# A new written-out order for the end of a one-core attention and maxout kernel, and five smaller final stores in place of four

## The chip, the core and the metric

The kernel runs on one core of a Trainium2 chip. The metric is the device time of one execution in microseconds (us), as the median of several runs. Engines are named as in the profile: PE (TensorE), DVE (VectorE), ACT (ScalarE), POOL (GpSimd) and SP (SyncE, which here only issues transfers). Each engine works through its own list of instructions in order.

## The reference

Attention with positive features for 8 batches of 8 heads, 576 tokens and head size 64, and after it a maxout layer on all 4608 tokens. Cut to what matters:

```
proj = einsum('bhsd,df->bhsf', x, w_phi); proj -= max(abs(proj), -1)
phi  = concat(exp(proj), exp(-proj))                 # for q and for k
attn = (q_p @ (k_p^T @ v)) / (q_p . sum(k_p) + 1e-6)
x    = attn as 4608 x 512
h    = maximum(maximum(x @ w1, x @ w2), x @ w3)      # 512 -> 768
out  = h @ w_out                                     # 768 -> 512, float32
```

## The kernel before

**The work.** The attention is made in 16 units (a batch and four of its heads each). Their results `xT` lie with the 512 channels on partitions, brought there by a transposing DMA (line 703). The maxout layer is done in nine blocks of 512 tokens (`chunk`, line 832): blocks 0 to 7 are the first 512 tokens of the batches, and block 8 is made of the last 64 tokens of all eight batches, which POOL copies together into `x_last` (line 965). The layer is rewritten: with the differences w2 - w1 and w3 - w1, h is x @ w1 + max(0, x @ (w2 - w1), x @ (w3 - w1)), so that the output is x @ (w1 @ w_out) + hT @ w_out.

**One block.** Six `up` and six `up2` products (line 848; 128 x 512 each, four matmuls) give the two differences for six slices of 128 hidden channels. An `up` result is clipped at zero out of PSUM into `hT` by ACT (line 857) or by DVE (line 859); an `up2` result is combined with it by a maximum on DVE (line 855). Then comes the output product, with an inner size of 512 + 768 = ten slices of 128.

**Blocks 5 to 8** make the output product with seven products of half size in place of eight (`fast`, line 742). POOL forms four sums or differences of quarters of x (128 x 512) and four of `hT` (128 x 768), all at line 760. PE then makes seven products p1 to p7 of ten matmuls each (line 795, 128 x 256), and the output block of 512 x 512 is put together out of PSUM: ACT or DVE copies p1 (line 808), and DVE makes seven additions (line 802) in the tiles `low` (tokens 0 to 255 of the block) and `high` (tokens 256 to 511), both of the pool `raw`, and in a temporary tile `osb`. A quarter is called c11 (low, columns 0 to 255), c12 (low, 256 to 511), c21 and c22 (high). The steps are: osb = p6 + p1; c21 = p7 + osb; c12 = p5 + osb, then + p3; c22 = p5 + c21; c21 = c21 + p4; c11 = p1 + p2. c22 must be made before p4 is added into c21.

**The stores.** The rows of blocks 0 to 7 leave as two DMAs of 64 x 512 float32 (128 KB) for each 128 tokens, all issued by SP; that is eight DMAs for a block. Block 8 leaves as four DMAs of 128 x 512 (256 KB), two issued by SP and two by ACT (line 827). A store waits for both column halves of its rows.

**The order.** Nothing is left to a scheduler when the program is built: every step (a node) has a number, and the string `PLAN` lists for each node its engine, a planned start and the buffer slots it takes (`154T5@38.05` is node 154 on PE in PSUM bank 5). `plan` (line 259) reads it, and each engine issues its nodes in that order. T is PE, D is DVE, A is ACT, G is POOL and S is SP. The planned starts only sort the steps; the engines wait for each other by semaphores. `fill` (line 277) puts idle matmuls into planned gaps of PE.

Of the kernel before, what the change touches and what calls it, by code (L numbers as in the profile page):

```python
# [233 lines left out]
1004T21@224.97 1050A@225.22 1058T4@225.29 1008T5@225.51 1005D0@225.54 1393G3@225.55 1051A@225.73 1064T160@225.93 1009D1@226.16
1060A@226.21 1059A@226.72 1061T7@227.06 1006T2@227.18 1056A@227.20 1066D@227.22 1391G5@227.28 1052T3@227.50 1065D@227.60
1002T4@227.72 1053A@227.97 1007D0@227.98 1353T5@228.04 1054A@228.47 1003D1@228.60 1062A@228.96 1392G@229.03 1399T0@229.13
1063A@229.32 1010S@229.37 1057A@229.66 1069T60@230.22 1073T2@230.54 1470G@230.76 1070D0@230.79 1071T3@230.86 1362S@230.87
1394G@231.16 1406T4@231.18 1072D1@231.43 1074D0@232.05 1067T7@232.27 1397T6@232.59 1068D1@232.84 1075S@233.61 1408T1@233.68
1395T3@234.77 1401T2@235.86 1396D0@236.11 1398D2@236.74 1404T7@236.95 1440G4@237.04 1409D@237.38 1400D7@238.00 1420T3@238.04
1472G@238.24 1403D@238.64 1497G5@238.66 1418T6@238.91 1407D@239.28 1477T1@239.78 1438G@239.86 1402D@239.90 1413S@240.05  # L240
1421D0@240.52 1422T0@240.65 1499G@241.06 1419D@241.13 1416T4@241.52 1423D@241.77 1439G@242.26 1405D@242.38 1424T2@242.39
1417A@242.64 1411S@243.15 1475T3@243.26 1498G@243.46 1425A@243.51 1436T6@244.13 1410S@244.35 1441G@244.66 1432T0@245.00
1412S@245.55 1500G@245.86 1489T7@245.87 1433D@246.12 1414T4@246.74 1437D@246.74 1434T0@247.61 1415A@247.86 1476A1@248.36
1426T2@248.48 1430T4@249.35 1427D@249.60 1491T6@250.22 1431D@250.47 1354D@251.09 1481T3@251.09 1435D@251.71 1359S@251.86
1428T2@251.96 1482A@252.21 1478D@252.33 1483T4@252.83 1360S@253.06 1429D@253.08 1487T5@253.70 1444G1@253.85 1484A@253.95
1361S@254.26 1493T0@254.57 1488D@254.82 1490D@255.44 1473T1@255.44 1442G3@255.58 1494D@256.06 1479T2@256.31 1474D@256.68
1495T3@257.18 1443G@257.33 1480A@257.43 1485T4@258.05 1492D@258.08 1450T5@258.92 1445G@259.08 1486D@259.17 1496D@259.79
1452T7@260.01 1501G0@260.81 1455T0@261.10 1459T1@262.19 1502G@262.56 1446T2@263.28 1503G1@264.29 1448T6@264.37 1447A7@264.62
1505T4@265.46 1449D0@265.71 1504G@266.02 1451D6@266.35 1457T3@266.55 1506A2@266.80 1460D@266.97 1454D@267.59 1511T2@267.64
1458D@268.23 1507T6@268.73 1453D@268.85 1464S@269.00 1456D@269.49 1509T5@269.82 1508D3@270.11 1463S@270.20 1512D@270.75  # L250
1516T1@270.91 1510D3@271.37 1462S@271.40 1518T4@272.00 1513D@272.01 1461S@272.60 1517D@272.65 1514T3@273.09 1519D@273.34
# [50 lines left out]
def kernel(  # L302
# [439 lines left out]
    def fast(b, ready, hT, evac, out_rows, ff, n_out):  # L742
# [46 lines left out]
        def product(a, w, s):
            ps = bank("fps", [P, 2, HF])  # L790

            def mm(ps=ps, a=a, w=w):
                for p in range(2):
                    for c in range(5):
                        nc.tensor.matmul(ps()[:, p, :], lhsT=a(c, p), rhs=w(c), start=(p + c == 0), stop=(p + c == 5))  # L795
# [4 lines left out]

        def add(ps, need, out, other, bufs):
            return ff("fa", {"DVE": 0.62}, lambda: nc.vector.tensor_tensor(out(), ps()[0](), other(), ALU.add),  # L802
                      need + [ps()[1]], [ps()[0]] + bufs, locks=[ps()[0]])
# [17 lines left out]
        n_11 = add(lambda: p2, [n_u], c11, c11, [low])
        for tt in range(SM // P):
            o2, need = (low, [n_11, n_12]) if tt < 2 else (high, [n_21, n_22])

            def store(n_, pieces, tt=tt, o2=o2):
                for dram_ap, rows in pieces:
                    queue_of[n_.eng].dma_start(dram_ap, o2()[rows, tt % 2, :])
# [183 lines left out]
```

## Time and profile before

| what | value |
|---|---|
| median of 3 runs | 282.27 us (281.68 to 282.67) |
| the profiled execution | 282.29 us, of which its span is 280.5 us |
| busy in the span: PE, DVE, ACT, POOL | 97%, 80%, 68%, 60% |
| granted PE clock | 0.996 of full speed |
| matmul instructions | 3663 |

The span runs from the first to the last instruction of the profiled execution, and 1.79 us of that execution's own time lie outside it. Times in the profile count from the start of the span. An instruction row gives start, duration, engine, line, and output<-input; a q behind an engine's name is its sequencer, which is busy while it issues a DMA. In rows of stretches, the columns are the busy time of each engine with the number of instructions begun there, then the granted clock of PE, the mean busy share of the 16 DMA engines, and GB/s.

### The profile page before, as it was taken

How to read it: one execution, taken by the hardware profiler on the slowest of the kernel's cores; microseconds unless marked ns; L12 is line 12 of the kernel's file. 1: busy time of each engine (PE TensorE's matmuls, PEld its weight loads, DVE VectorE, ACT ScalarE, POOL GpSimd, SP SyncE). 2: the span in 40 equal slices, each digit the busy share in tenths (PEclk: the TensorE clock that was granted, in tenths of full speed). 3: DMA queues.
4: the chain of work that ended last, by engine and by line, in shares of the span. 5: the costliest groups of instructions: out<-in, count | busy, mean ns of one | idle time of the engine just before them, and what ended most of it. 6: DMA issues, size and time to landing. Idle time of an engine off the chain costs nothing.

```text
span 280.5 us, 8829 instructions
## 1 busy us (share of the span) xinstructions
PE 270.9 (97%) x3663; PEld 164.1 (58%) x3663; DVE 224.0 (80%) x466; ACT 191.3 (68%) x439; POOL 168.5 (60%) x147
## 2 busy tenths in 40 slices
PE   8899999999999999999999999999999999999991
PEld 3566774465546555564556456565485589444881
DVE  4899899988869997889898878897589565756292
ACT  3799997798879988898684699887654860112000
POOL 8075787839444764570768079267875892927910
PEclk9999999999999999999999999999999999999998
DMA  7999999997999997799899729984232108245037
GB/s 212 234 211 320 266 224 197 384 277 139 287 382 245 197 313 251 193 204 227 240 263 156 194 49 261 202 201 89 51 78 49 40 18 118 55 95 116 0 89 212
DMA packets 68050, 51.46 MB, mean 183 GB/s; under 512 B 48746, under 2 KB 52650, under 8 KB 68010
## 3 DMA queue, kind: packets, MB, share of 16 engines
q1 hardware_dynamic: 63561, 45.41, 66.2%
q0 software_dynamic: 4000, 4.92, 10.3%
q8 instruction: 28, 0.46, 0.6%
q10 hardware_dynamic: 449, 0.57, 0.6%
q14 instruction: 12, 0.10, 0.1%
HBM read 34.64 MB, written 9.44 MB: 157 GB/s over the span
## 4 chain that ended last, share of the span: by engine, by line
PE 78%; DMA 9%; DVE 6%; ACT 3%; issue 1%; POOL 1%; DVEq 0%; POOLq 0%; ACTq 0%
PE ups L848 33%; PE fps L795 8%; PE ops L884 7%; PE psn L673 5%; PE kvps L655 5%; PE ops L879 5%; PE psq L547 5%; PE psm L626 5%; DMA qk_bf<-in_k_dram 3%; DMA qkT<-qk_bf 3%; DMA qkT<-mT 3%; ACT Eq L639 2%; DVE raw L802 2%; PE pm L950 2%; PE tps L509 1%; DVE mqp L566 1%
## 5 line engine op out<-in xcount | busy, mean ns | idle before, releaser
L601 POOL TENSOR_TENSOR vab<-raw,em 128x1152 bf16<-128x1152 f32 (+1 forms) x36 | 68.1, 1906 | 69.4 <-ACT em L597 55.1
L560 ACT ACTIVATE Ek<-psk 128x512 bf16<-128x512 f32 (+1 forms) x160 | 82.2, 568 | 13.8 <-PE psk L547 10.0
L848 PE MATMUL ups<-xT,w_bf 128*128 128x512 bf16 x384 | 90.8, 379 | 0.0
L639 ACT ACTIVATE Eq<-psm 128x512 bf16<-128x512 f32 (+1 forms) x160 | 79.4, 571 | 10.4 <-PE psm L626 9.6
L848 PEld LDWEIGHTS <-w_bf 128*128 128x128 bf16 x432 | 41.0, 98 | 46.4
L566 DVE TENSOR_REDUCE mqp<-psq 128x4 bf16<-128x512 f32 (+1 forms) x80 | 49.2, 634 | 8.4 <-PE psk L547 5.7
L566 DVE TENSOR_REDUCE mk<-psk 128x4 f32<-128x512 f32 (+1 forms) x80 | 48.9, 630 | 1.1 <-ACT Ek L560 0.5
L855 DVE TENSOR_TENSOR hT<-hT,ups 128x512 bf16<-128x512 bf16 x54 | 36.2, 684 | 16.8 <-PE ups L848 13.9
L857 ACT ACTIVATE hT<-ups 128x512 bf16<-128x512 f32 x28 | 16.6, 606 | 30.1 <-PE ups L848 30.0
L680 DVE TENSOR_TENSOR x_sb<-psn,rden 128x320 bf16<-128x320 f32 x64 | 31.5, 492 | 2.2
L492 POOL CAST qk_bf<-raw 128x1152 bf16<-128x1152 f32 x24 | 27.2, 1148 | 5.8 <-DMA qkT<-qk_bf 3.5
L673 PEld LDWEIGHTS <-Eq 128*128 128x128 bf16 x640 | 24.7, 97 | 7.5 <-ACT Eq L639 0.7
L884 PE MATMUL ops<-wout_bf,hT 128*128 128x512 bf16 x120 | 29.1, 379 | 0.0
L673 PE MATMUL psn<-kv_sb,Eq 128*128 128x65 bf16 x640 | 26.8, 194 | 0.5 <-ACT Eq L639 0.5
L547 PE MATMUL psq<-w,qkT 64*128 64x128 bf16 x288 | 24.5, 217 | 1.0 <-DMA qkT<-qk_bf 0.6
L547 PE MATMUL psk<-w,qkT 64*128 64x128 bf16 x288 | 24.1, 217 | 0.2
L547 PEld LDWEIGHTS <-qkT 64*128 64x128 bf16 x576 | 16.6, 94 | 12.7 <-issue 8.9
L626 PE MATMUL psm<-qkT,wphi_m 128*128 128x512 bf16 (+1 forms) x70 | 22.3, 359 | 0.5 <-DMA qkT<-mT 0.3
L879 PE MATMUL ops<-xT 128*128 128x512 bf16 x80 | 20.6, 380 | 0.0
L859 DVE TENSOR_SCALAR hT<-ups 128x512 bf16<-128x512 f32 x26 | 17.5, 684 | 3.8 <-PE ups L848 3.6
L655 PE MATMUL kvps<-vab,Ek 64*128 64x65 bf16 x1152 | 20.2, 190 | 0.0
L655 PEld LDWEIGHTS <-Ek 64*128 64x128 bf16 x1152 | 18.8, 94 | 2.3 <-DVE mk L566 0.4
(97 smaller groups left out, 333.8 us busy)
## 6 DMA issues: line engine op xcount, KB each, us to landing
raw<-in_v_dram SPq DMA_DIRECT2D x16, 576.0 KB
raw<-in_q_dram SPq DMA_DIRECT2D x12, 576.0 KB
raw<-in_k_dram SPq DMA_DIRECT2D x12, 576.0 KB
out_dram<-osb SPq DMA_DIRECT2D x40, 128.0 KB
out_dram<-raw SPq DMA_DIRECT2D x24, 128.0 KB
w_bf<-in_moe_w_dram POOLq DMA_DIRECT2D x3, 768.0 KB, 9.4
qk_bf<-in_q_dram POOLq DMA_DIRECT2D x3, 288.0 KB, 8.2
qk_bf<-in_k_dram POOLq DMA_DIRECT2D x3, 288.0 KB, 9.3
```

Of the source, the lines that this page charges most:

```text
L547: nc.tensor.matmul(ps()[:, i, :], lhsT=cols[r, :], rhs=w2[r, c, :], start=True, stop=True)
L560: nc.scalar.activation(Ek[s]()[:, tiles_of(t0, n), :], of(1), EXP, scale=1.0 - 2.0 * s)
L566: nc.vector.tensor_reduce((mq, mk)[c]()[:, tiles_of(t0, n)], of(c), AXX, ALU.max, apply_absolute_value=True)
L601: (nc.vector if n_.eng == "DVE" else nc.gpsimd).tensor_tensor(vab()[:, g, t0:t1, 0:D], vb()[:, t0:t1, :], em()[:, g, t0:t1].unsqueeze(2).t ...
L626: nc.tensor.matmul(psm()[:, 0:w], lhsT=wphi_m, rhs=rhs, start=True, stop=True)
L639: nc.scalar.activation(Eqb()[s][:, cols], psm()[:, 0:w], EXP, scale=1.0 - 2.0 * s)
L655: nc.tensor.matmul(kvps[ab]()[:, t // NT, g, :], lhsT=Ek[g]()[r, t, :], rhs=vab()[r, g, t, :], start=(t + g == 0), stop=(t == UT - 1 and g ...
L673: nc.tensor.matmul(psn()[:, c, :], lhsT=Eqb()[g][:, t0:t0 + P], rhs=kv()[:, pr, ab, g, :], start=(g == 0), stop=(g == 1))
L848: nc.tensor.matmul(ups(), lhsT=w_bf[i + 1][:, ct, j * P:(j + 1) * P], rhs=tokens_of(ct), start=(ct == 0), stop=(ct == CT - 1))
L855: nc.vector.tensor_tensor(hT()[:, j, :], hT()[:, j, :], ups(), ALU.max)
L879: nc.tensor.matmul(ops_()[:, 0:width], lhsT=tile_of(ct, tt), rhs=line_w[:, ct, cols], start=(ct == 0), stop=False)
L884: nc.tensor.matmul(ops_()[:, 0:width], lhsT=hT()[:, j, tt * P:(tt + 1) * P], rhs=wout_bf[:, j, cols], start=False, stop=(j == JT - 1))
```

## The change

The change writes the plan anew from 225 us on (orders and buffer slots), and divides the end of block 8. In earlier parts of the string only three pairs of nodes with equal or nearly equal starts on different engines change places. There are three kinds of edits:

- The order of blocks 7 and 8. Before, their `up` and `up2` products were mixed; now block 7 is finished first, `up` and `up2` alternate, and all twelve clips out of PSUM are on ACT (before, ACT had seven of them and DVE five). Block 7's seven products come as p1 (ahead of the last `up2` of block 8), p6, p5, p3, p2, p7, p4, and block 8's as p1, p2, p6, p7, p5, p3, p4 (before p1, p5, p6, p7, p4, p2, p3).
- In block 8, p4 is made as two products of five matmuls, one for each 128 tokens, in two PSUM banks, and is added to c21 in two additions of 128 x 256.
- Block 8 leaves in five DMAs by column halves: c11, c12 and c22 as 128 x 2 x 256 (256 KB in rows of 1 KB), and c21 as two of 128 x 256 (128 KB). Each waits for its own additions alone.

```diff
-1522A@273.42 1523S@273.80 1515D@274.43 1520S@275.20 1521A@275.20
+1518T1@273.82 1515D@273.84 1524A@273.99 1517D@274.53 1523S@274.68 1519D@274.95 1525A@275.10 1526S@275.52
...
-        def product(a, w, s):
-            ps = bank("fps", [P, 2, HF])
+        def product(a, w, s, halves=(0, 1)):
+            ps = bank("fps", [P, len(halves), HF])
...
-                for p in range(2):
+                for k, p in enumerate(halves):
                     for c in range(5):
-                        nc.tensor.matmul(ps()[:, p, :], lhsT=a(c, p), rhs=w(c), start=(p + c == 0), stop=(p + c == 5))
+                        nc.tensor.matmul(ps()[:, k, :], lhsT=a(c, p), rhs=w(c), start=(k + c == 0),
+                                         stop=(k == len(halves) - 1 and c == 4))
...
-        p4 = product(a_of(1, 1), t_of(3), None)
-        n_21 = add(lambda: p4, [n_7, n_22], c21, c21, [high])
+        n_21 = []
+        for halves in ((0,), (1,)) if b == B else ((0, 1),):
+            p4 = product(a_of(1, 1), t_of(3), None, halves)
+
+            def c21_of(halves=halves):
+                return high()[:, halves[0]:halves[-1] + 1, 0:HF]
+            n_21.append(add(lambda p4=p4: p4, [n_7, n_22], c21_of, c21_of, [high], 0.07 + 0.28 * len(halves)))
...
-        for tt in range(SM // P):
-            o2, need = (low, [n_11, n_12]) if tt < 2 else (high, [n_21, n_22])
+        parts = [(low, 0, 2, 0, HF, n_11), (low, 0, 2, HF, DM, n_12), (high, 0, 2, HF, DM, n_22),
+                 (high, 0, 1, 0, HF, n_21[0]), (high, 1, 2, 0, HF, n_21[-1])]
+        for o2, p0, p1_, c0, c1, need in parts if b == B else []:
+            def last(n_, o2=o2, p0=p0, p1_=p1_, c0=c0, c1=c1):
+                whole = out.rearrange("(r c) n -> c r n", c=NT)[NT - 1]
+                t0 = HT * (o2 is high)
+                queue_of[n_.eng].dma_start(whole[t0 + p0 * P:t0 + p1_ * P, c0:c1].rearrange("(t p) n -> p t n", p=P),
+                                           o2()[:, p0:p1_, c0:c1])
+            n_ = ff("store", {"SP": 0.6, "ACT": 0.6}, None, [need], [o2], pipe=0.5 * (p1_ - p0), lat=1.5, packet=100.0)
+            n_.fn = lambda n_=n_, f=last: f(n_)
+        for tt in range(0 if b == B else SM // P):
+            o2, need = (low, [n_11, n_12]) if tt < 2 else (high, n_21 + [n_22])
```

DVE's last seven additions before, all of block 8. Here raw_5731 is `low`, raw_5789 is `high` and osb_5773 the temporary; the fps tiles are the products in PSUM:

```order
L802 TENSOR_TENSOR osb_5773<-fps_5747,raw_5731 128x512
L802 TENSOR_TENSOR raw_5731<-fps_5735,osb_5773 128x2x256
L802 TENSOR_TENSOR raw_5789<-fps_5762,osb_5773 128x2x256
L802 TENSOR_TENSOR raw_5789<-fps_5735,raw_5789 128x2x256
L802 TENSOR_TENSOR raw_5789<-fps_5778,raw_5789 128x2x256
L802 TENSOR_TENSOR raw_5731<-fps_5793,raw_5731 128x2x256
L802 TENSOR_TENSOR raw_5731<-fps_5808,raw_5731 128x2x256
```

DVE's last eight now, with raw_5751 as `low`, raw_5793 as `high` and osb_5779 as the temporary:

```order
L803 TENSOR_TENSOR osb_5779<-fps_5755,raw_5751 128x512
L803 TENSOR_TENSOR raw_5751<-fps_5740,raw_5751 128x2x256
L803 TENSOR_TENSOR raw_5793<-fps_5768,osb_5779 128x2x256
L803 TENSOR_TENSOR raw_5751<-fps_5782,osb_5779 128x2x256
L803 TENSOR_TENSOR raw_5793<-fps_5782,raw_5793 128x2x256
L803 TENSOR_TENSOR raw_5751<-fps_5796,raw_5751 128x2x256
L803 TENSOR_TENSOR raw_5793<-fps_5809,raw_5793 128x256
L803 TENSOR_TENSOR raw_5793<-fps_5815,raw_5793 128x256
```

c11 (the addition of p2) has moved from the sixth place to the second, and the last two rows are the two halves of c21 in place of c11 and c12.

SP's last stores before; raw_5718 and raw_5702 are `high` and `low` of block 7, raw_5789 and raw_5731 those of block 8, and the first two rows belong to blocks 5 and 6:

```order
L827 DMA out_0_dram<-raw_4799 64x512 x4
L827 DMA out_0_dram<-raw_4903 64x512 x2
L827 DMA out_0_dram<-raw_5718 64x512 x4
L827 DMA out_0_dram<-raw_5702 64x512 x4
L827 DMA out_0_dram<-raw_5789 128x512
L827 DMA out_0_dram<-raw_5731 128x512
```

The same place now, where raw_5641 and raw_5722 are `low` and `high` of block 7, and raw_5751 and raw_5793 those of block 8:

```order
L843 DMA out_0_dram<-raw_4799 64x512 x4
L843 DMA out_0_dram<-raw_4903 64x512 x2
L843 DMA out_0_dram<-raw_5641 64x512 x4
L843 DMA out_0_dram<-raw_5722 64x512 x4
L834 DMA out_0_dram<-raw_5751 128x2x256 x2
L834 DMA out_0_dram<-raw_5793 128x256
```

The eight stores of block 7 stay ahead of SP's stores of block 8, which are now c11, c12 and the second half of c21. ACT's last two instructions were stores of 128 x 512 and are now c22 (128 x 2 x 256) and the first half of c21 (128 x 256).

POOL before, from its last copy into `x_last` on, with the sums for block 7 (from xT) and block 8 (from x_last) and then those of both from hT:

```order
L965 COPY x_last<-xT 128x4x64
L760 TENSOR_TENSOR raw<-x_last 128x512
L760 TENSOR_TENSOR raw<-xT 128x512
L760 TENSOR_TENSOR raw<-x_last 128x512
L760 TENSOR_TENSOR raw<-raw,xT 128x512
L760 TENSOR_TENSOR raw<-raw,x_last 128x512
L760 TENSOR_TENSOR raw<-xT,raw 128x512
L760 TENSOR_TENSOR raw<-x_last,raw 128x512
L760 TENSOR_TENSOR raw<-hT 128x768 x2
L760 TENSOR_TENSOR raw<-raw,hT 128x768
L760 TENSOR_TENSOR raw<-hT,raw 128x768
```

The same place now:

```order
L981 COPY x_last<-xT 128x4x64
L760 TENSOR_TENSOR raw<-xT 128x512
L760 TENSOR_TENSOR raw<-raw,xT 128x512
L760 TENSOR_TENSOR raw<-xT 128x512
L760 TENSOR_TENSOR raw<-xT,raw 128x512
L760 TENSOR_TENSOR raw<-x_last 128x512
L760 TENSOR_TENSOR raw<-raw,x_last 128x512
L760 TENSOR_TENSOR raw<-x_last 128x512
L760 TENSOR_TENSOR raw<-x_last,raw 128x512
L760 TENSOR_TENSOR raw<-hT 128x768
L760 TENSOR_TENSOR raw<-raw,hT 128x768
```

One sum of block 7 that stood ahead of the copy now stands behind it, and block 7's four come before block 8's.

More of the change, by code (lines that the diff above doesn't have):

```diff
@@ L117 @@
 147D0@35.90 135A@36.26 152T7@36.41 76D1@36.52 197G@36.68 193T1@36.73 136A@36.77 153D0@37.14 84A@37.25 150T0@37.40 81T6@37.72
-199A@37.90 151D1@37.97 194A0@38.05 154T5@38.05 189A@38.30 233T2@38.36 195S@38.45 82D@38.59 180A@38.64 364G@38.78 156T7@38.81
+199A@37.90 151D1@37.97 154T5@38.05 194A0@38.05 189A@38.30 233T2@38.36 195S@38.45 82D@38.59 180A@38.64 364G@38.78 156T7@38.81
 234D@39.06 155A@39.13 363S1@39.15 242T111011@39.21 215T064@39.45 297S2@39.61 245D@39.70 157A@39.78 366S1@40.07 1082D@40.31
@@ L132 @@
 376D@59.70 429G1@59.81 378A@60.02 269T5@60.03 380D@60.30 387T43@60.35 270A@60.51 281T6@60.56 1125T@60.68 391D@60.91 271A@61.02
-381D@61.25 283A@61.50 390D@61.86 282A@61.86 218T0@61.98 1126A1@62.23 278T5@62.30 291T61@62.52 219D1@62.55 395A0@62.84
-289T4@62.84 279A@63.09 287T1@63.16 292D0@63.17 397G0@63.24 226S@63.32 1136T0@63.48 280A@63.59 290D1@63.79 388A@64.08 293T5@64.35
+381D@61.25 283A@61.50 390D@61.86 282A@61.86 218T0@61.98 1126A1@62.23 278T5@62.30 291T61@62.52 219D1@62.55 289T4@62.84
+395A0@62.84 279A@63.09 287T1@63.16 292D0@63.17 397G0@63.24 226S@63.32 1136T0@63.48 280A@63.59 290D1@63.79 388A@64.08 293T5@64.35
 288D0@64.41 379A@64.42 1132T6@64.67 389A@64.91 294D1@65.03 374A@65.25 398G@65.33 430G@65.61 312T114211@65.63 295S@65.80
@@ L149 @@
 1139S@88.43 343T2@88.54 351D@88.76 421T3@88.76 754G2@88.93 345A@89.01 334T4@89.08 337T1@89.30 422D1@89.33 356T71@89.52
-496S2@89.77 338A@89.77 423T5@89.84 357D0@90.09 1165T@90.16 339A@90.28 446D@90.71 335A@90.76 689G@90.86 344A@91.25 424D1@91.32
+338A@89.77 496S2@89.77 423T5@89.84 357D0@90.09 1165T@90.16 339A@90.28 446D@90.71 335A@90.76 689G@90.86 344A@91.25 424D1@91.32
 419T3@91.46 336A@91.73 354T1@91.78 420D0@92.03 358T7@92.10 444A@92.22 1168T2@92.42 355D1@92.65 1166A2@92.71 425S@92.97
@@ L233 @@
 1388G@223.08 1033A@223.49 1383T7@223.66 1380D@223.91 1038A@223.98 1390G@224.30 1055T10@224.53 1049T3@224.75 1384D@224.78
[L234 to L251, printed above, removed]
-1522A@273.42 1523S@273.80 1515D@274.43 1520S@275.20 1521A@275.20
+1004T21@224.97 1050A@225.41 1058T4@225.48 1008T6@225.70 1005D0@225.73 1393G3@225.74 1051A@225.91 1064T150@226.11 1009D1@226.35
@@ new lines @@
+1060A@226.40 1059A@226.90 1061T7@227.25 1006T2@227.37 1056A@227.39 1066D@227.40 1391G5@227.47 1052T3@227.69 1065D@227.78
+1002T6@227.91 1053A@228.16 1007D0@228.16 1353T4@228.23 1054A@228.66 1003D1@228.78 1062A@229.15 1392G@229.22 1399T0@229.32
+1063A@229.51 1010S@229.55 1057A@229.85 1069T50@230.41 1073T2@230.73 1470G@230.95 1070D0@230.98 1071T3@231.05 1362S@231.05
+1394G@231.35 1406T6@231.37 1072D1@231.62 1074D0@232.24 1067T7@232.46 1397T1@232.78 1068D1@233.03 1075S@233.80 1408T5@233.87
+1395T3@234.96 1401T2@236.05 1396D0@236.30 1398D2@236.93 1404T7@237.14 1472G@237.23 1409D@237.57 1438G7@237.63 1400D4@238.19
@@ new lines @@
+1414T3@238.23 1403D@238.83 1439G@238.85 1416T1@239.10 1415A0@239.35 1407D@239.47 1426T5@239.97 1440G@240.05 1402D@240.10
+1417A@240.22 1413S@240.25 1418T0@240.84 1427D@241.09 1441G@241.25 1405D@241.71 1428T3@241.71 1419A@241.96 1497G5@242.45
+1411S@242.48 1420T6@242.58 1429D@242.83 1430T2@243.45 1498G@243.67 1410S@243.68 1421A@243.70 1422T1@244.32 1431D@244.57
+1499G@244.87 1412S@244.88 1432T5@245.19 1423A@245.44 1424T7@246.06 1500G@246.07 1433D@246.31 1434T0@246.93 1425A@247.18
+1473T3@247.80 1435D@248.05 1436T6@248.67 1474A1@248.92 1475T2@249.54 1437D@249.79 1354D@250.41 1485T1@250.41 1442G1@250.56
@@ new lines @@
+1476A@250.66 1359S@251.18 1477T5@251.28 1486D@251.53 1487T7@252.15 1443G@252.31 1360S@252.38 1478A@252.40 1479T0@253.02
+1488D@253.27 1361S@253.58 1489T3@253.89 1445G3@254.06 1480A@254.14 1481T6@254.76 1490D@255.01 1491T4@255.63 1444G@255.79
+1482A@255.88 1483T2@256.50 1492D@256.75 1493T1@257.37 1484A@257.62 1446T5@258.24 1494D@258.49 1495T7@259.33 1447A0@259.58
+1448T0@260.20 1496D@260.45 1501G4@261.22 1452T3@261.29 1449D3@261.54 1455T6@262.38 1453D@262.63 1502G@262.97 1459T4@263.47
+1456D@263.72 1450T2@264.56 1503G6@264.70 1460D@264.81 1457T1@265.65 1461S@265.65 1451D2@265.90 1504G@266.43 1454D@266.61
@@ L253 @@
+1505T5@266.74 1462S@266.85 1458D@267.32 1520T7@267.83 1506A1@268.08 1463S@268.17 1507T0@268.92 1464S@269.37 1509T6@270.01
+1508D0@270.26 1521D@270.97 1511T4@271.10 1510D3@271.66 1522S@271.81 1514T2@272.19 1512D@272.44 1513D@273.15 1516T3@273.28
+1518T1@273.82 1515D@273.84 1524A@273.99 1517D@274.53 1523S@274.68 1519D@274.95 1525A@275.10 1526S@275.52
 """
@@ L787, in fast, with add @@
         base = ready + evac + lines + [w_nodes[3]] + t_made
-        def product(a, w, s):
-            ps = bank("fps", [P, 2, HF])
+        def product(a, w, s, halves=(0, 1)):
+            ps = bank("fps", [P, len(halves), HF])
             def mm(ps=ps, a=a, w=w):
-                for p in range(2):
+                for k, p in enumerate(halves):
                     for c in range(5):
-                        nc.tensor.matmul(ps()[:, p, :], lhsT=a(c, p), rhs=w(c), start=(p + c == 0), stop=(p + c == 5))
+                        nc.tensor.matmul(ps()[:, k, :], lhsT=a(c, p), rhs=w(c), start=(k + c == 0),
+                                         stop=(k == len(halves) - 1 and c == 4))
             need = [] if s is None else [made[0, s], made[1, s]]
-            n_ = ff("fp", {"PE": 1.09}, mm, base + need, [hT, ps] + ([] if s is None else [Sx, Sr[s // 2]]))
+            n_ = ff("fp", {"PE": 0.545 * len(halves)}, mm, base + need, [hT, ps] + ([] if s is None else [Sx, Sr[s // 2]]))
             readers[b].append(n_)
             return ps, n_
-        def add(ps, need, out, other, bufs):
-            return ff("fa", {"DVE": 0.62}, lambda: nc.vector.tensor_tensor(out(), ps()[0](), other(), ALU.add),
+        def add(ps, need, out, other, bufs, dve=0.62):
+            return ff("fa", {"DVE": dve}, lambda: nc.vector.tensor_tensor(out(), ps()[0](), other(), ALU.add),
                       need + [ps()[1]], [ps()[0]] + bufs, locks=[ps()[0]])
```

## The prediction

> **What bounds the kernel now.** I read the page's head, then busy times by stretch, the chain that ended last, the timeline of the end, and the DMA share there. The page shows an engine that is nearly always busy:
>
> ```profile
> span 280.5 us, 8829 instructions
> PE 270.9 (97%) x3663; PEld 164.1 (58%) x3663; DVE 224.0 (80%) x466; ACT 191.3 (68%) x439; POOL 168.5 (60%) x147
> ```
>
> The stretches show where it isn't (up and up2 products of blocks 7 and 8, then their half-size products, then the end):
>
> ```profile
> 220.00:238.30 18.30, 18.30 (x265) 14.66 (x264) 10.96 (x26) 8.82 (x20) 13.29 (x12) 1.00 0.43 67
> 238.30:259.20 20.90, 20.90 (x100) 9.57 (x98) 13.64 (x22) 4.07 (x7) 13.20 (x12) 1.00 0.39 89
> 259.20:274.60 15.40, 15.39 (x141) 13.54 (x139) 9.58 (x15) 1.17 (x2) 7.98 (x5) 1.00 0.24 55
> 274.60:280.50 5.90, 0.00 (x0) 0.00 (x0) 0.73 (x2) 0.00 (x0) 0.00 (x0) 0.80 0.67 213
> ```
>
> PE is full from 220 us to 274.6 at a granted clock of 1.00. Busy time of overlapping matmuls could hide slack, so I check the pace in the chain of waits:
>
> ```profile
> 238.58 20.72 PE ups L848 x96
> 259.30 6.56 PE fps L795 x60
> ```
>
> That is 0.216 us for each of 96 matmuls of 512 columns and 0.109 for each of 60 of 256: half the columns at half the time, so nothing waits. Hence a new order cannot shorten the part before 274.6; it can only open holes. What can shrink is the end, 280.5 - 274.6 = 5.9 us. Its timeline:
>
> ```profile
> 269.40 1.10 SPq L827 DMA_DIRECT2D out_dram<-raw  x2
> 274.09 0.49 PE L795 MATMUL fps<-wout_bf,raw 128*128 128x256 bf16 x3
> 274.05 1.28 DVE L802 TENSOR_TENSOR raw<-fps,raw 128x512 f32<-128x512 f32 x2
> 274.17 0.36 ACTq L827 DMA_DIRECT2D out_dram<-raw  x1
> 274.46 0.53 SPq L827 DMA_DIRECT2D out_dram<-raw  x1
> 275.36 0.49 SPq L827 DMA_DIRECT2D out_dram<-raw  x1
> 275.36 0.36 ACTq L827 DMA_DIRECT2D out_dram<-raw  x1
> ```
>
> PE's last result is there at 274.09 + 0.49 = 274.58, DVE's last addition ends at 274.05 + 1.28 = 275.33, and two stores of 256 KB are issued 0.03 later. What the DMA engines do meanwhile (the last two columns are busy share and GB/s), and how long SP waits after its last issue:
>
> ```profile
> 269.40:270.50 1.10, 1.10 (x13) 0.99 (x11) 1.06 (x2) 0.00 (x0) 0.00 (x0) 1.00 0.00 0
> 270.50:274.10 3.60, 3.60 (x36) 3.22 (x34) 3.43 (x7) 0.00 (x0) 0.00 (x0) 1.00 0.90 205
> 274.10:275.70 1.60, 0.49 (x5) 0.19 (x2) 1.23 (x3) 0.00 (x0) 0.00 (x0) 1.00 0.93 181
> 275.70:278.80 3.10, 0.00 (x0) 0.00 (x0) 0.00 (x0) 0.00 (x0) 0.00 (x0) 0.89 0.95 345
> 278.80:280.50 1.70, 0.00 (x0) 0.00 (x0) 0.00 (x0) 0.00 (x0) 0.00 (x0) 0.50 0.00 0
> SPq L1006 <- DMA out_dram<-raw: 3.2, 1, 3.2
> ```
>
> Block 7's eight stores go out from 269.4 and, 64 partitions each, move at 205 GB/s with the engines 90% busy: 1.05 MB / 205 is 5.1 us, so they last until past 275.7. Only then does block 8's megabyte get the engines, until 278.8. The end is a DMA backlog, and 1.7 us from its last byte to the end of the span.
>
> **The change, part by part.** *The order before 274.6.* The matmuls are the same, so PE's floor stays: 0. Cover for the moved steps: the five clips that go from DVE to ACT join an engine with much idle time, and the sums on POOL keep their count.
>
> ```profile
> L857 ACT ACTIVATE hT<-ups 128x512 bf16<-128x512 f32 x7 | 4.1, 596 | 23.7 <-PE ups L848 23.7
> 239.05 1.15 POOL L760 TENSOR_TENSOR raw<-x_last 128x512 bf16<-128x512 bf16 x1
> 259.34 1.29 DVE L855 TENSOR_TENSOR hT<-hT,ups 128x512 bf16<-128x512 bf16 x2 [0.41 <-PE ups L848]
> 260.70 1.64 POOL L760 TENSOR_TENSOR raw<-hT 128x768 bf16<-128x768 bf16 x1
> 265.61 1.65 POOL L760 TENSOR_TENSOR raw<-hT,raw 128x768 bf16<-128x768 bf16 x1
> ```
>
> Twelve clips are 12 x 0.6 = 7.2 us in a stretch of 20.9. The one with consumers behind it is POOL: its eight sums of x begin at 239.05 whatever the order (one now comes later, 8 x 1.15 = 9.2, until 248.3), block 7's maxima are complete after the 13th up or up2 product, at about 238.4 + 13 x 0.863 + 0.9 = 250.5 (0.863 is 4 x 0.216), and block 7's four sums of hT take until 250.5 + 4 x 1.68 = 257.2. (Before: 260.70 to 265.61 + 1.65 is 4 in 6.56, with waits; I take 1.68 each.) Block 8's last maximum now has a product of 1.09 us (10 x 0.109) ahead of it, so its four sums start near 261.2 and end near 267.9. PE needs two of them for p6, which starts at 274.5 - 5 x 1.09 = 269.0, when they have been done for 4 us. No hole follows.
>
> *Block 7's stores.* Block 7's first two quarters are now complete after its p2, and all after its p4. Counted back from 274.5, nine products of blocks 7 and 8 (p7 and p4, then block 8's seven) come after that p2, so p2 ends at 274.5 - 9 x 1.09 = 264.7; after an addition (0.69) SP can issue from about 265.5, 3.9 us earlier than 269.4. 64-partition traffic then ends near 265.5 + 1.1 + 5.1 = 271.7, before block 8's first store. The 5.1 us are unchanged; they now lie beside products.
>
> *DVE's end.* Prices, from the groups of instructions:
>
> ```profile
> L802 DVE TENSOR_TENSOR raw<-fps,raw 128x512 f32<-128x512 f32 x14 | 9.4, 687 | 1.1 <-PE fps L795 0.6
> L680 DVE TENSOR_TENSOR x_sb<-psn,rden 128x320 bf16<-128x320 f32 x8 | 3.9, 492 | 0.3
> ```
>
> 192 columns more cost 195 ns, so a half of 256 columns is about 492 - 65 = 0.43 us. p5, p3 and the two halves of p4 are ready at 272.4, 273.5, 274.05 and 274.6. Additions follow each other at about 0.64 us (274.05 + 1.28 less a last one of 0.68 leaves 0.60; dependent ones take 0.70). The two additions of p5 start at 272.45 and 273.1, that of p3 at 273.75, those of p4 at 274.4 and 274.8. So c22 is complete at 273.8, c12 at 274.4, c21's halves at 274.8 and 275.2. DVE itself gains 0.1 (0 to 0.25, since p4's last half can't start before 274.6).
>
> *Block 8's stores.* c11 is out of the way: complete near 271.6, its 256 KB are moved before c22 comes. Each store waits for its additions at the head of its queue; behind c11's stand only c12's and c21's second half on SP, and behind c22's only c21's first half on ACT, all due later than what they stand behind, so these waits hold up nobody. SP's first store at 269.40 has its first bytes at 270.50, 1.1 us on. For ACT the queues of two stretches (274.17 to 275.70, and 275.70 to 276) and prices of packets in two more (276 to 278, rows of 2 KB; 2.6 to 3.4, the load of w_phi in rows of 512 bytes):
>
> ```profile
> q1 hardware_dynamic: 167, 0.28, 92.9%
> q10 hardware_dynamic: 16, 0.03, 29.8%
> q10 hardware_dynamic: 236, 0.45, 58.2%
> q10 hardware_dynamic: 80, 0.03, 14.6%
> ```
>
> Only q1, SP's queue, moved anything before 275.70; so ACT's store (q10) took 1.5 us from 274.17. With 1.5 us, c22's bytes start at 275.3, and from there the engines have work without a break: c12 is due at 274.4 + 1.1 = 275.5, c21's halves at 276.3. That is 768 KB, or 768 packets of 1 KB, 48 for each engine. A packet of 1 KB does not occur alone here. Bounds: 236 packets of 1.9 KB took 0.582 x 16 x 2 / 236 = 79 ns each, so 84 for 2 KB; 80 of 0.4 KB took 0.146 x 16 x 0.8 / 80 = 23 ns. Below, half of 84, 42 ns; above, 84, if size doesn't matter. On the line through both rows 1 KB costs 46 ns, which I take, since the two rows lie on either side of it. 48 x 46 ns = 2.2 us: the last byte lands at 277.5 to 277.55 instead of 278.8, 1.25 us earlier. The 1.7 us behind it stay.
>
> The Trainium skill, SBUF — State Buffer, section The DMA setup-cost knee, gives a transfer about 2 us fixed plus its bytes at 436 GB/s. By that the last 128 KB, issued at 275.25, would release SP at 277.55, which is 1.5 us before the 279.1 of the trace, and the sum would come to 280.8; the trace's own last store took 3.7 us (275.36 to 279.1), where the fit has 2.6, so queueing, which it leaves out, is what the row shows on top.
>
> *Sum.* 282.29 (the profiled execution, 0.02 from the median of 282.27) - 1.25 = 281.04, say 281.0. Ends: with ACT as quick as SP (c22's bytes from 274.9) and 42 ns, the last byte is at about 277.1, bound by c21's second half, and the time 280.6; with 84 ns, 275.3 + 4.0 = 279.3, and 282.8.
>
> **The rivals.** A measurement of this kernel can tell about 0.3%, 0.85 us, so faster is below 281.4 and slower above 283.1.
>
> *Short rows eat it.* A packet of 1 KB that costs 54 to 90 ns puts the last byte between 277.9 and 279.6, and the time between 281.4 and 283.1: no difference that can be told. Against it: 23 ns for 0.4 KB. For it: no row of this size. The Trainium skill, Perfetto Trace Analysis, section DMA Optimizations, speaks for this rival: DMAs under 2 KB have a significant overhead each and should be batched into larger ones; it gives no price, and the trace bears it out only weakly, with 23 ns for a fifth of the bytes of a 79 ns packet.
>
> *Slower: the stores of two rows per partition move like the 64-partition ones.* Those have a row of their own (271 to 274):
>
> ```profile
> q1 hardware_dynamic: 379, 0.61, 89.2%
> ```
>
> 0.61 MB are 299 packets of 2 KB; 0.892 x 16 x 3 / 299 = 143 ns each. If a packet of 1 KB of block 8 cost that, 48 x 143 ns = 6.9, the last byte would be at 282.2 and the time at 285.7. It turns slower from 90 ns on. Against it: the same block's stores over 128 partitions took 84 ns for twice the bytes.
>
> *A hole in PE.* If POOL's sums of block 8 came over 4 us later than I count, or a PSUM bank were not free, PE would stand and the whole hole be added; a hole of 1.25 us would make no difference (282.3), one of 2.1 slower. The banks' owners in the new plan are read at least 1.7 us before their next use by the durations above.
>
> *The split does nothing*, because a store still waits for the rest of its tile: then `low` is released at 274.4 and `high` at 275.2, a megabyte (64 packets for each engine, 2.9 us) moves from 275.5, the last byte lands at 278.4, and the time is 281.9. Each new store has its own count of DVE's steps to wait for, which speaks against it.
>
> **How the numbers follow.** Forecast 0.68, at 281.0, by itself 280.6 to 281.4. Short rows 0.17 and no split 0.05, both between 281.4 and 283.1. A hole 0.07, half of it same, half slower. Slow rows 0.03, slower. So faster 0.68, same 0.25 (0.17 + 0.05 + 0.03), slower 0.07. The range takes in the forecast's lower end, 0.2 below it for the spread of the runs, and the greater part of the short rows: 280.4 to 282.3.
>
> **What would show it.** Right: PE full to 274.6; block 7's stores from about 265.5; no DMA traffic shortly before 272; c22 issued near 273.8 and the last store near 275.25; last bytes near 277.5; 1.7 us after them. Wrong: a wait of PE between 238 and 274, a last addition after 275.4, or DMA engines that are busy until 278.5 with only 768 KB to move.

## The result and the profile after

| | before | changed |
|---|---|---|
| median of 15 runs each | 282.96 us (281.68 to 284.46) | 281.61 us (280.41 to 282.26) |
| the profiled execution | 282.29 us, span 280.5 | 282.20 us, span 280.4 |
| PE's last result, in the span | 274.58 | 276.25 |
| from there to the end of the span | 5.9 us | 4.2 us |

The ratio of the times is 0.9943, with a 95% interval of 0.9925 to 0.9961: faster by 1.6 us, between 1.1 and 2.1. The forecast was 1.25 us less, at 281.0; the difference of the medians is 1.35. The time itself came out 0.6 us above the forecast because the base did: 282.96 over 15 runs, where the three runs that the forecast started from had 282.27.

The two profiled executions do not show that gain in their spans, so the first thing is to see where it is. The head of the page and the stretches of the changed kernel (columns as before):

```profile
span 280.4 us, 8845 instructions
PE 271.9 (97%) x3663; PEld 164.5 (59%) x3663; DVE 221.8 (79%) x462; ACT 194.6 (69%) x444; POOL 168.3 (60%) x147
```

```profile
238.30:259.20 20.90, 20.90 (x107) 10.28 (x106) 12.51 (x19) 6.57 (x11) 15.87 (x13) 1.00 0.40 91
259.20:274.60 15.40, 15.40 (x136) 13.06 (x134) 8.69 (x13) 1.77 (x3) 6.48 (x4) 1.00 0.32 73
274.60:276.25 1.65, 1.65 (x16) 1.23 (x13) 1.65 (x4) 0.00 (x0) 0.00 (x0) 1.00 0.38 129
276.25:278.79 2.54, 0.00 (x0) 0.00 (x0) 0.46 (x2) 0.00 (x0) 0.00 (x0) 1.00 0.90 310
278.79:280.40 1.61, 0.00 (x0) 0.00 (x0) 0.00 (x0) 0.00 (x0) 0.00 (x0) 0.60 0.00 0
```

PE is full here too, but until 276.25 and not 274.58. Did the new order open holes? The chain of waits of the changed kernel says no:

```profile
234.78 5.46 PE fps L795 x50
240.24 19.86 PE ups L864 x92
260.10 1.09 PE fps L795 x10
261.19 0.86 PE ups L864 x4
262.06 12.02 PE fps L795 x110
```

Each piece begins where the last one ended, at 0.216 us for a matmul of 512 columns and 0.109 for one of 256, as before. The 1.67 us are there ahead of the first piece. The same piece of five products in the chain of the kernel before:

```profile
233.12 5.46 PE fps L795 x50
```

234.78 - 233.12 = 1.66: this execution was late before any instruction of the rewritten end had begun. (The eighth experiment shows the same program part beginning at 233.12 in the new order.) So the two ends are compared from PE's last result on, which I call the tail: 280.5 - 274.58 = 5.9 us before, 280.4 - 276.25 = 4.15 now, 1.75 us less. By the second decimal of the trace they are 5.92 and 4.16, and in that form the tails stand in the table of the experiments.

The timeline of the end: sums of hT on POOL (the first and last of block 8's four), stores, and the last additions.

```profile
262.93 1.64 POOL L760 TENSOR_TENSOR raw<-hT 128x768 bf16<-128x768 bf16 x1 [3.93 <-DVE hT L871]
267.18 5.01 SPq L843 DMA_DIRECT2D out_dram<-raw  x8
267.84 1.64 POOL L760 TENSOR_TENSOR raw<-hT,raw 128x768 bf16<-128x768 bf16 x1
273.50 3.58 SPq L834 DMA_DIRECT2D out_dram<-raw  x3
274.71 2.00 DVE L803 TENSOR_TENSOR raw<-fps,raw 128x512 f32<-128x512 f32 x4
275.42 1.28 ACTq L834 DMA_DIRECT2D out_dram<-raw  x2
```

What the DMA engines do between these rows:

```profile
268.20:273.50 5.30, 5.30 (x51) 4.74 (x50) 2.83 (x6) 0.58 (x1) 1.29 (x1) 1.00 0.89 198
273.60:274.20 0.60, 0.60 (x8) 0.54 (x6) 0.57 (x2) 0.00 (x0) 0.00 (x0) 1.00 0.00 0
274.20:275.40 1.20, 1.20 (x13) 1.08 (x12) 1.20 (x3) 0.00 (x0) 0.00 (x0) 1.00 0.64 219
275.40:276.30 0.90, 0.85 (x8) 0.51 (x6) 0.90 (x3) 0.00 (x0) 0.00 (x0) 1.00 0.00 0
276.30:278.80 2.50, 0.00 (x0) 0.00 (x0) 0.41 (x2) 0.00 (x0) 0.00 (x0) 1.00 0.92 315
```

Block 7's stores move from 268.3 to 273.6, all beside products; c11 moves alone between 274.2 and 275.4; then the engines stand idle until c22's bytes come at 276.3, 0.9 us after its issue at 275.42. From there 768 KB go out almost without a gap and are done at 278.79, 2.54 us after PE's last result (4.2 us before). 1.6 us follow them.

### The profile page after: what moved, and what is told of

The parts are those of the page before. It is cut to its first block, busy times and chain, and to the rows that moved or that the text cites. A ratio compares the mean times of both kernels' runs of the same rounds, so it can differ in the third digit from the quotient of the medians.

```text
span 280.4 us, 8845 instructions
## 1 busy us (share of the span) xinstructions
PE 271.9 (97%) x3663; PEld 164.5 (59%) x3663; DVE 221.8 (79%) x462; ACT 194.6 (69%) x444; POOL 168.3 (60%) x147
## 4 chain that ended last, share of the span: by engine, by line
PE 68%; DMA 11%; ACT 8%; DVE 5%; POOL 3%; issue 2%; SPq 1%; POOLq 0%; ACTq 0%
PE ups L864 28%; PE fps L795 10%; PE kvps L655 5%; PE ops L900 5%; PE psn L673 4%; PE psm L626 4%; PE ops L895 4%; PE psq L547 4%; DMA qk_bf<-in_k_dram 4%; ACT Eq L639 3%; ACT Ek L560 3%; DMA xT<-x_sb 3%; DMA raw<-in_v_dram 2%; DMA qkT<-mT 2%; DVE x_sb L680 2%; PE pm L966 2%
## 5 line engine op out<-in xcount | busy, mean ns | idle before, releaser
L873 ACT ACTIVATE hT<-ups 128x512 bf16<-128x512 f32 x33 | 19.7, 605 | 27.4 <-PE ups L864 27.2
L760 POOL TENSOR_TENSOR raw<-hT 128x768 bf16<-128x768 bf16 x8 | 13.1, 1638 | 8.0 <-DVE hT L871 8.0
```

## The experiments

The theory was that the tail is set by the DMA engines: block 7's stores hold them, block 8's wait, and the gain is made of the backlog taken away, the stores by quarters and the split of p4. The rivals give the gain to one part alone, or to DVE's earlier end. In the texts on record a tail counts from PE's last result, and A stands for the theory. All kernels ran beside the kernel before: the first four beside 35 runs of it (median 282.95), the others beside 23 (282.70). Each was profiled once, so a tail is that of one execution. In all six experiments with an interval, the ratio that the tail's difference would give lies inside it; the intervals are too wide to rank the parts by time alone.

**The new order alone.** The whole new plan up to the last product, with p4 and the stores of block 8 as before (shown against the changed kernel, without the lines of the plan):

```diff
-        for halves in ((0,), (1,)) if b == B else ((0, 1),):
...
+        p4 = product(a_of(1, 1), t_of(3), None)
+        n_21 = add(lambda: p4, [n_7, n_22], c21, c21, [high])
...
+        for tt in range(SM // P):
+            o2, need = (low, [n_11, n_12]) if tt < 2 else (high, [n_21, n_22])
```

> The new order of steps with the old stores: block 8 leaves as four DMAs of 128 x 512, p4 is one product, and each store waits for both column halves. The tail is the time from PE's last result to the end of the span: 5.92 us before, 4.15 in the changed kernel. Theory A (a DMA backlog, both parts needed): block 7's traffic is gone, but low's megabyte half can only leave after c12 and high's after the whole of c21, which ends 0.73 after PE; its 512 KB in rows of 2 KB (84 ns each, 1.34 us) then follow low's and end near +3.4, tail 5.0 to 5.1, time 0.3% under before. Rival B (the order alone is the gain, the form of the stores doesn't matter): tail 4.2 to 4.4, time 0.6% under before. Rival C (only the form of the stores matters): tail 5.9, time as before. Rival D (rows of 1 KB cost more than they bring): tail under 4.15.

Measured: ratio 0.9979 (0.9954 to 1.0003), median 282.12. The stretches from PE's last result on:

```profile
276.09:279.65 3.56, 0.00 (x0) 0.00 (x0) 0.69 (x1) 0.00 (x0) 0.00 (x0) 1.00 0.78 295
279.65:281.10 1.45, 0.00 (x0) 0.00 (x0) 0.00 (x0) 0.00 (x0) 0.00 (x0) 0.89 0.00 0
```

The tail is 5.0 us: the order alone is worth 0.95 of the 1.76. The DMA engines are busy 78% of the first stretch, where before they were busy 93 to 95%, since with block 7 out of the way they wait for the last additions. Rival D (a tail under 4.15) fell too: with rows of 2 KB the tail is longer, not shorter.

**The new stores alone.** Before's order, with block 8 stored by quarters (p4 in one piece):

```diff
-1522A@273.42 1523S@273.80 1515D@274.43 1520S@275.20 1521A@275.20
+1522A@272.80 1523A@273.43 1520S@274.11 1515D@274.43 1521S@275.20
...
+        parts = [(low, 0, 2, 0, HF, n_11), (low, 0, 2, HF, DM, n_12), (high, 0, 2, HF, DM, n_22),
+                 (high, 0, 2, 0, HF, n_21[0])]
```

> The order of before with block 8's stores by quarters (c11, c12, c22, c21, each 128 x 2 x 256, each waiting for its own additions; p4 not divided). c22 is complete 1.2 us before PE's end and c21 0.45 before, but block 7's 64-partition traffic holds the DMA engines until about 1.2 after it. Theory A: the same megabyte still has to follow that traffic, in packets of 46 ns (64 per engine, 2.9 us), last byte near +4.0, tail 5.6 to 5.7, time at most 0.1% under before. Rival B: tail 5.9. Rival C: tail 4.2 to 4.4 and time 0.6% under before.

Measured: ratio 1.0025 (0.9998 to 1.0052), median 283.67: no gain. The stores, the stretch from PE's last result at 274.70 to the last byte, and the packets from the issue of c22 to 275.0 (first row: SP's queue, the only one) and those of ACT's queue in the microsecond after it:

```profile
269.51 4.99 SPq L843 DMA_DIRECT2D out_dram<-raw  x8
273.48 1.21 ACTq L834 DMA_DIRECT2D out_dram<-raw  x2
```

```profile
274.70:278.93 4.23, 0.00 (x0) 0.00 (x0) 0.74 (x2) 0.00 (x0) 0.00 (x0) 1.00 0.99 299
```

```profile
q1 hardware_dynamic: 176, 0.30, 95.1%
q10 hardware_dynamic: 172, 0.18, 55.9%
```

c22 is issued on ACT at 273.48, and until 275.0 only q1, SP's queue with block 7's bytes, moves anything. The engines are busy 99% of the 4.23 us from PE's last result to the last byte. A's tail of 5.6 to 5.7 was a miss: it let the earlier issue count for something. With this backlog the end was the sum of all bytes that were left; leaving earlier in smaller pieces only changed whose bytes went first.

**No split.** The changed kernel with p4 in one piece and c21 in one store, from SP:

```diff
-        for halves in ((0,), (1,)) if b == B else ((0, 1),):
+        for halves in ((0, 1),):
...
-                 (high, 0, 1, 0, HF, n_21[0]), (high, 1, 2, 0, HF, n_21[-1])]
+                 (high, 0, 2, 0, HF, n_21[0])]
```

> The changed kernel with p4 and c21 in one piece: one product of ten matmuls, one addition of 128 x 512, one store of 256 KB in place of two of 128 KB. Theory A: the last addition starts when PE ends and ends at +0.73 instead of +0.46, the store is issued at +0.76, its first bytes move at +1.85 when the engines have just finished c12, and its 256 KB take 0.75: last byte at +2.6 against +2.54, tail 4.2 to 4.3, no difference in the time. Rival (the split is worth a good part of the gain): tail 4.6 or more, time 0.15% or more over the changed kernel's.

Measured: ratio 0.9957 (0.9933 to 0.998), median 281.59.

```profile
276.05:278.61 2.56, 0.00 (x0) 0.00 (x0) 0.69 (x1) 0.00 (x0) 0.00 (x0) 0.90 0.91 307
```

The last addition ends 0.27 us later than with the split (0.73 against 0.46 after PE's last result), and the last byte 0.02: the engines still had other bytes to move. The split is worth 0.1 us of tail and nothing that the times show.

**No backlog.** The kernel before without block 7's eight stores; the 512 rows of block 7 are not written:

```diff
             def store(n_, pieces, tt=tt, o2=o2):
+                if b == B - 1:
+                    return
                 for dram_ap, rows in pieces:
```

> The kernel before without block 7's eight stores: those 512 rows of the output are not written, everything else is. It prices the backlog alone. Theory A: block 8's first store on ACT moves its bytes about 1 us after its issue, not 1.5, the four stores' 512 packets of 2 KB (32 per engine, 2.7 us) run from +0.5 to +3.2, tail 4.8 to 4.9, time 0.35% under before. Rival (no backlog: the end is the latency of the last stores): tail 5.8 to 5.9, time as before.

Measured: ratio 0.9962 (0.9941 to 0.9984), median 281.69.

```profile
276.40:279.36 2.96, 0.00 (x0) 0.00 (x0) 0.35 (x1) 0.00 (x0) 0.00 (x0) 0.89 0.95 354
279.36:280.80 1.44, 0.00 (x0) 0.00 (x0) 0.00 (x0) 0.00 (x0) 0.00 (x0) 0.50 0.00 0
```

PE's last result is at 276.00, so the tail is 4.8 us, 1.1 less than with the stores. Nothing else was changed (with eight issues fewer, SP also issues block 8's first store 0.3 us sooner, counted from PE's last result): the backlog of these stores is shown as a cause, and as the greater part of the gain.

**Quarters without a backlog.** The kernel of the new stores alone, with the same `return`:

> The kernel of the quarter stores in the old order (before's plan, block 8 stored by quarters), with block 7's eight stores left out, so that block 7's 512 rows of the output are not written. It fills the fourth corner: order old or new, backlog there or not, quarters or whole rows. Theory A (the quarters did nothing in the old order only because block 7's traffic still held the DMA engines): c22 is issued near -1.2 us counted from PE's last result, its bytes come near -0.3, and the last of the four, c12, issued at +0.77, has its last byte at +2.7 to +2.9; the tail is 4.3 to 4.6 us, against 4.82 with whole rows. Rival B (the quarters help only with the new order of the last additions, since in the old one the last two quarters are complete at the very end): last byte +3.2 to +3.4 and a tail of 4.7 to 4.9, as without the quarters.

One execution, 281.47 us. The issue of ACT's stores, the stretch in which c22's bytes begin, and the one from PE's last result to the last byte:

```profile
273.78 1.17 ACTq L834 DMA_DIRECT2D out_dram<-raw  x2
```

```profile
274.70:275.00 0.30, 0.30 (x3) 0.02 (x1) 0.30 (x1) 0.00 (x0) 0.00 (x0) 1.00 0.90 314
275.00:277.95 2.95, 0.00 (x1) 0.00 (x0) 0.74 (x2) 0.00 (x0) 0.00 (x0) 0.93 0.97 324
```

The last byte came at +2.95, 0.4 us earlier than with whole rows (+3.36), and the tail is 4.65 (only 0.2 shorter, since 1.7 us follow the last byte here and 1.44 there): between the two theories' ranges and just outside A's. The same store of c22 on the same queue had its first bytes 0.9 us after its issue (273.78 to 274.70), where behind block 7's bytes it took 1.6 (273.48 to 275.05 in the kernel of the new stores alone): nothing but the backlog was taken away between the two. The quarters do work once the backlog is gone, but by less than A had it; in the old order the last two quarters are complete at the very end, and their 512 KB lie behind that. With the new order of the additions and the same four stores (the kernel without the split) the tail was 4.25.

**The new kernel without block 7's stores.** The changed kernel with the same `return`:

> The changed kernel without block 7's eight stores (its 512 rows of the output are not written). Theory A (the new order hides them wholly beside products): the tail stays at 4.1 to 4.25 us, the last byte at +2.5 to +2.6 from PE's last result, and the ratio to the kernel before is that of the changed kernel, 0.993 to 0.997. Rival B (their last traffic, which ends 2.6 us before PE's last result, still delays block 8's stores): last byte at +2.1 to +2.35, tail 3.8 to 4.0 us.

Measured: ratio 0.9957 (0.9936 to 0.9978), median 281.56.

```profile
274.69:277.23 2.54, 0.00 (x0) 0.00 (x0) 0.46 (x2) 0.00 (x0) 0.00 (x0) 1.00 0.90 310
```

The same 2.54 us at the same 310 GB/s as with the stores: the new order hides them wholly.

**c22 first.** An attempt to start the last stream earlier: of the two additions of p5, that of c22 comes first.

```diff
-1514T2@272.19 1512D@272.44 1513D@273.15 1516T3@273.28
+1514T2@272.19 1513D@272.44 1512D@273.15 1516T3@273.28
```

> The changed kernel with one exchange on DVE: of the two additions of p5, that which completes c22 comes first, that towards c12 second. Theory A (what is left of the tail is the stream of the last 768 packets of 1 KB, which starts when c22's store has its first bytes): c22 is issued 0.6 us earlier, near -1.4 from PE's last result, its bytes come from -0.5; 48 packets per engine at 47 ns are 2.26 us, so the stream would end at +1.8, and the last addition's own path then decides: issue +0.49, first bytes 1.1 later, 128 KB in 0.37, last byte +1.96 to +2.1. Tail 3.6 to 3.75 us, ratio to the kernel before 0.991 to 0.994. Rival B (the last quarter's own path is what ends last already, or a gap opens between c22's bytes and c12's that eats it): last byte +2.4 to +2.6, tail 4.0 to 4.2, ratio 0.993 to 0.996.

Measured: ratio 0.996 (0.9932 to 0.9988), median 281.55. The additions and ACT's stores, and the DMA share after them:

```profile
271.83 0.68 DVE L803 TENSOR_TENSOR raw<-fps,osb 128x512 f32<-128x512 f32 x1
272.62 0.69 DVE L803 TENSOR_TENSOR raw<-fps,raw 128x512 f32<-128x512 f32 x1
273.22 0.68 DVE L803 TENSOR_TENSOR raw<-fps,osb 128x512 f32<-128x512 f32 x1
273.34 2.07 ACTq L834 DMA_DIRECT2D out_dram<-raw  x2
274.01 1.35 DVE L803 TENSOR_TENSOR raw<-fps,raw 128x512 f32<-128x512 f32 x3
```

```profile
274.30:275.00 0.70, 0.39 (x4) 0.10 (x1) 0.70 (x3) 0.00 (x0) 0.00 (x0) 1.00 0.98 339
275.00:275.45 0.45, 0.00 (x0) 0.00 (x0) 0.36 (x2) 0.00 (x0) 0.00 (x0) 1.00 0.13 39
275.45:277.29 1.84, 0.00 (x0) 0.00 (x0) 0.00 (x0) 0.00 (x0) 0.00 (x0) 1.00 0.83 285
```

Rival B: c22 is issued 1.35 us ahead of PE's last result (274.69) instead of 0.83, and its bytes are nearly through by 275.0, but then the engines stand nearly idle for 0.45 us, and the last byte is at +2.60. The second addition to c12 now stands right behind the first, whose result it reads: 274.01 - 273.22 = 0.79 us from start to start, where additions that don't depend on each other took 0.60 (273.22 - 272.62). That is 0.19 us; c22's addition, too, now stands right behind the one whose result it reads (272.62 - 271.83 = 0.79). So c12 and all behind it came 0.2 to 0.3 us later. In the changed kernel the addition of c22 lies between the two to c12 and covers that distance. No version tried has a tail more than 0.03 us shorter than the changed kernel's.

**Queues exchanged.** The changed kernel with c22 and c21's first half on SP, and c12 and c21's second half on ACT:

```diff
-1524A@273.99 1517D@274.53 1523S@274.68 1519D@274.95 1525A@275.10 1526S@275.52
+1524S@273.99 1517D@274.53 1523A@274.68 1519D@274.95 1525S@275.10 1526A@275.52
```

> The changed kernel with the queues of its last four stores exchanged: c22 and c21's first half from SP, c12 and c21's second half from ACT. Theory A (the time from an issue to the first bytes is about 0.9 to 1.1 us on either queue when the DMA engines are idle, and the 1.5 us that the prediction took for ACT held only beside block 7's traffic): c22's bytes from +0.1 to +0.3 from PE's last result, c12's from ACT by +0.9, the last byte at +2.5 to +2.7, the tail 4.1 to 4.3 us. Rival B (ACT's queue is the slower one, 1.5 us whatever the engines do): c12's first bytes at +1.2 to +1.4, a gap behind c22's, last byte +2.8 to +3.0, tail 4.4 to 4.6 us.

One execution, 280.52 us, PE's last result at 274.58; the chain has the five products at 233.12, as before the change. ACT's stores; the DMA share; and the packets of ACT's queue from 274.60 to 275.30 (none are listed) and from 275.30 to 276.00, beside SP's in both:

```profile
274.35 1.07 ACTq L834 DMA_DIRECT2D out_dram<-raw  x2
```

```profile
274.30:274.60 0.30, 0.28 (x3) 0.00 (x0) 0.30 (x2) 0.00 (x0) 0.00 (x0) 1.00 0.00 0
274.60:274.90 0.30, 0.00 (x0) 0.00 (x0) 0.30 (x2) 0.00 (x0) 0.00 (x0) 1.00 0.77 270
274.58:277.09 2.51, 0.00 (x1) 0.00 (x0) 0.46 (x2) 0.00 (x0) 0.00 (x0) 1.00 0.91 313
```

```profile
q1 hardware_dynamic: 207, 0.21, 90.7%
q10 hardware_dynamic: 188, 0.19, 80.4%
q1 hardware_dynamic: 65, 0.05, 22.0%
```

c22 from SP (issued 0.83 us ahead of PE's last result, at 273.75) has its first bytes 0.9 us later; c12 from ACT, issued at 274.35, begins a little after 275.30, 1.0 to 1.1 us on. The last byte is at +2.51 and the tail 4.1 us, as in the changed kernel. So theory A: about 1 us on either queue, with the engines idle (c22) or with the 256 KB of one store under way (c12), and 1.6 behind block 7's backlog, as in the kernel of the new stores alone.

**Together.** Tails in us, from PE's last result to the end of the span:

| block 8's stores | old order | old order, block 7 not stored | new order | new order, block 7 not stored |
|---|---|---|---|---|
| whole rows | 5.92 (before) | 4.82 | 4.97 | |
| quarters | 5.93 | 4.65 | 4.25 | |
| quarters, p4 split | | | 4.16 (changed) | 4.17 |

Along the table, 1.1 of the 1.76 us is the backlog, 0.2 the quarters, 0.4 the order of the last additions, which lets the quarters become complete one after the other, and 0.1 the split. The parts do not add up in any order: the quarters are worth 0.0 in the old order and 0.7 in the new one, and with whole rows the new order's tail (4.97) is even 0.15 longer than that of the old order without block 7's stores (4.82).

## Why the prediction was right, step by step

- **PE has no slack ahead of the end, and the new order opens no hole**: right, by the chain above. Shifted by the 1.66 us, block 8's sums of hT run from 261.3 to 267.8 (forecast 261.2 to 267.9).
- **Block 7's stores move beside products**: right. Shifted, their issues begin at 265.5 (forecast 265.5) and their traffic ends at 271.9 (271.7). The two kernels without these stores show that this was the cause in the old order and costs nothing in the new.
- **DVE's end**: right; half additions took 0.41 us (forecast 0.43), and the last ended 0.46 us after PE's last result (forecast 0.6). The 0.70 us for dependent additions stand at the low end of what the traces show: 0.71 to 0.79 from start to start.
- **The first bytes of c22: the term that was mis-sized.** "With 1.5 us, c22's bytes start at 275.3" would be +0.7 from PE's last result; they came at +0.1, 0.9 us after the issue. The 1.5 had been read off a store that was issued into block 7's traffic, and the prediction's own next step was that this traffic is gone by then. Its lower end, "with ACT as quick as SP", was the case.
- **1 KB packets at 46 ns**: nearly. From 276.3 to 277.0 of the changed kernel ACT's queue is alone:

```profile
q10 hardware_dynamic: 207, 0.21, 90.4%
```

That is 0.904 x 16 x 0.7 / 207 = 49 ns. The whole stream took 2.44 us instead of 2.2. The two errors go against each other. So the last byte is 0.6 - 0.2 = 0.4 us earlier than forecast, and 1.6 us follow it and not 1.7: 1.25 + 0.4 + 0.1 = 1.75 is what the tails show.
- **The rival of the short rows** fell: 49 ns is below the 54 from which it would have decided. Rows of 2 KB at 84 ns would have moved 768 KB in 384 x 84 / 16 = 2.0 us, so short rows cost 0.3 us of the tail and save more. The Trainium skill, Perfetto Trace Analysis, section DMA Optimizations, counts small DMAs, under 2 KB, as burdened with a significant overhead each; read for the packets of a DMA, as the prediction did, the trace bears that out by 7 ns for each packet of 1 KB (49 less half of 84).
- **The rival of the slow rows** fell with the same row, **that of a split that does nothing** with the stores, which left at times of their own (c22 at 275.42, c12 at 276.01, c21's halves at 276.35 and 276.74).
- **The fixed cost of the last store.** After its last issue, which ends at 276.01 + 1.07, SP waits for DMAs:

```profile
276.01 1.07 SPq L834 DMA_DIRECT2D out_dram<-raw  x2
```

```profile
SPq L1022 <- DMA out_dram<-raw: 1.9, 2, 1.6
```

The two waits end at 279.13: 2.4 us after the issue of the last store (276.74, 0.34 before the end of that row), for 128 KB; before, it was 3.8 for 256 KB (275.36 to 279.16; the prediction has 3.7). The Trainium skill, SBUF — State Buffer, section The DMA setup-cost knee, has 2 us and the bytes at 436 GB/s, by which I estimate 2.3 here. The 2.4 are near it, but no clean test: c12's 256 KB moved ahead of these bytes on the same queue, from 277.09. The test of the prediction's reading, that the rest of the 3.7 was queueing, is the kernel before without block 7's stores:

```profile
SPq L1008 <- DMA out_dram<-raw: 2.3, 1, 2.3
```

SP's last store of 256 KB is issued at 276.78 there, and this wait ends at 279.48, after 2.7 us instead of 3.8. So 1.1 us of the 3.8 were block 7's backlog.
- **The sum.** The time of 281.0 came from a base of 282.29. The base of 15 runs is 282.96, the changed kernel's 281.61. The forecast change of 1.25 lies in the measured 1.1 to 2.1, and so does the tails' 1.76; the runs don't tell these two apart. The prediction's bound for faster, 281.4, was 0.85 us under its base; against the base of 15 runs the same bound is 282.1, and 281.61 lies below it. That 281.61 also lies in the stated range of times is partly luck, since the base moved by 0.67 us, half of the forecast gain.

What stays open is why one execution comes to 233.1 us and another to 234.8 at the same instruction. It doesn't go with the order: of the six profiled kernels in the new order, three had PE's last result at 274.58 to 274.69 and three at 276.05 to 276.25, and in the old order it lay at 274.58, 274.70, 275.00 and 276.00. Three of the four late ones were profiled in the first set of four experiments, none in the second. The traces show one place where part of it arises. In the three late ones of the new order PE stands at one product near 191 us, behind a step on POOL. The rows of the kernel without the split, where POOL had waited for a load of v:

```profile
187.19 2.12 POOL L601 TENSOR_TENSOR vab<-raw,em 128x1152 bf16<-128x1152 f32 x1 [10.01 <-DMA raw<-in_v_dram]
191.59 1.28 PE L655 MATMUL kvps<-vab,Ek 64*128 64x65 bf16 x72 [1.53 <-POOL vab L601]
```

PE stands 1.53 us here, 1.08 in the new order alone and 0.50 in the changed kernel, and at most 0.32 in the other seven executions. Set against the kernel before by the starts of ACT's instructions, the lateness grows at this place from 0.17 to 1.46 us, from 0.67 to 1.50 and from 1.40 to 1.66. So it arose here for the greater part in two of the three, and in the changed kernel mostly ahead of it (0.6 us by 16 us). What makes POOL's step late in some executions stays open; no experiment changed it, and the spread is as large as the gain.

## What to carry to other kernels

When PE is full to its last result, measure the tail from there, and ask what the DMA engines do in its first microseconds: if older stores keep them busy, pull these ahead first: here that was worth more than cutting the last ones up, and cutting them up was worth nothing until it was done. Take the time from an issue to its first bytes from a store that stands as the changed one will, behind other bytes or not. Compare two profiled executions by stages, since a spread ahead of the change can hide all of it.

## What the runs showed of the hardware

- Packets of 1 KB over 128 partitions cost 49 ns and those of 2 KB 84, where 2 KB from 64 partitions cost 143: block 7's stores from 64 partitions moved 198 to 205 GB/s, block 8's 310 to 354.
- A store had its first bytes 0.9 to 1.1 us after its issue on both queues, with idle engines or beside one store of 256 KB on the other queue, and 1.6 us behind block 7's eight stores.
- An addition on DVE that reads the result of the one right before it started 0.71 to 0.79 us after that one's start (271.93 to 272.65 before the change; 273.22 to 274.01 with c22 first), and one that touches other quarters 0.60 (128 x 512 out of PSUM). What decides between 0.71 and 0.79 was not looked into.
- From the last byte to the end of the span it took 1.6 to 1.7 us with stores by quarters, and 1.44 in the two kernels with whole rows and no backlog. The difference lies between the last byte and the end of SP's wait for the stores, 0.3 us in the changed kernel (278.79 to 279.13) and 0.1 in the kernel before without block 7's stores (279.36 to 279.48); from there on both took 1.3 us. Why the first piece differs was not looked into.
